# Clamp inside the adding instruction and half-size products for tokens 1024 to 1535, in a windowed-attention and two-layer kernel

## The chip, the core and the metric

The kernel runs on one core of one Trainium2 chip. The engines that it uses are PE (TensorE: matrix products and transposes), DVE (VectorE), ACT (ScalarE), POOL (GpSimd, here only for issuing loads that convert to bf16) and SP (SyncE, here for issuing transposing transfers and stores). They run side by side, each through its own list of instructions in order, and wait for each other by semaphores. The metric is the device time of one execution in microseconds (us). Lower is better.

## The reference

Attention in a window of 32 positions to either side, for 8 batches of 8 heads, 576 positions and 64 values a head; then two dense layers over the 4608 tokens of width 512, with a squared relu between them.

```
scores = 1/sqrt(64) * q @ k^T ;  |i - j| > 32 masked out
attn = softmax(scores) ;  x = attn @ v          # x: 4608 tokens x 512
h = x @ w_in                                     # w_in 512 x 2048
g = max(h, 0) ** 2
out = g @ w_out                                  # w_out 2048 x 512
```

Inputs and output are fp32; the kernel computes in bf16 with fp32 sums.

## The kernel before

**Attention.** The tokens come in 24 groups G of 192 (three groups, g = 0 to 2, to a batch b). For each group POOL loads q and k (`load_qk`, line 377: the tile `raw`, four buffers, so that group G and group G + 4 use the same one) and v (`load_v`, line 415). q and k have to be turned, so that the head's 64 values lie across partitions. For G below `NTG` PE turns them (`turn_pe`, line 463: eight small transposes for k and eight for q) and DVE or ACT brings them from PSUM to the tile `kq`; for the others SP issues a transposing transfer from `raw` to `kq` (`turn_dma`, line 491: two for a group, `td` and the group's numbers in the names). Then `scores` (line 531, PE; for G below `NSPLIT` the two halves of a group are issued apart), the exponential on ACT (line 554), the mask on DVE (562), `pv` (line 590, PE: two halves `P..A` and `P..B` of eight matmuls each) with a reciprocal and a normalising product on DVE (604, 608), and `xturn`, which turns the result for the first layer: by PE for G below `NXT` (lines 630 and 636, four transposes each, and a copy into the tile `xt`), otherwise by two transposing transfers of SP (lines 649 and 652, `T..a` and `T..b`).

**First layer.** Tokens 0 to 1023 go in tiles of 192 or 256 tokens through `mm1` (line 690). Tokens 1024 to 1535 (`PAIR`) go through `mm1` too, 16 outputs of 128 features for all 512 tokens at once, each of four matmuls of 512 columns; two outputs share two PSUM banks, one relu of 1024 elements a partition and one square of 1024. From 1536 on (`MM1S`) each set of 512 tokens goes through `mm1s`. There the product is split in two by two by two and made by seven products of half the size in place of eight (Strassen's scheme in Winograd's form). Four blocks m of features, each: seven products of four matmuls of 256 columns (line 770, named `Q<token>.<m><product>`), a seed copy within PSUM (line 809), four evictions by ACT or DVE (two relus, two plain copies to fp32 tiles `oe`), two adds of PSUM and such a copy (line 794), a clamp of both sums at zero (lines 800, 801) and squares (lines 659, 660) that write the tile `gt`. The products need sums of quarters of w_in (tile `sw`, made once, line 730) and differences of quarters of `xt` (tile `xs`, four per token set, line 742).

**Second layer.** Tokens 0 to 511 go by plain matmuls (`mm2`, line 835). The later sets of 512 go by seven products as well (`strassen`, line 917: products of 16 matmuls of 256 columns, named `P<set>.<product><half>`), with sums of `gt` on DVE (line 885), copies and adds (669, 670, 949) and stores that SP or ACT issues (847, 848).

**What sets the order.** A planner outside the kernel has given every operation a start number in nanoseconds; the long text `ORDER` holds them in the order in which the operations are recorded, with a letter for the engine (P for PE, A for ACT, D for DVE, G for POOL, S for SP), and after them the buffer of each tile. `apply` sorts by these numbers. The kernel does not wait for the times; only the order within each engine, the engine chosen and the buffer follow from them. Many operations may be given to ACT or to DVE. `fill` puts small idle matmuls in front of PE's early work (line 299). `OPEN` lists the first loads.

Of the kernel before, what the change touches and what calls it, by code (L numbers as in the profile page):

```python
# [2 lines left out]

# [12 lines left out]
RING = 1536  # L16
# [5 lines left out]
    MM1S=(1536, 2048, 2560, 3072, 3584, 4096),  # L22
# [8 lines left out]
    NTG=9,  # L31
# [3 lines left out]
    NXT=9,  # L35
    NSPLIT=6,
# [20 lines left out]
    ALTB=300,  # L57
)
# [174 lines left out]
class Gen:  # L233
# [7 lines left out]
    def alloc(self):  # L241
# [159 lines left out]
    def load_v(self, b, g, key, after=None):  # L401
        G, NV = 3 * b + g, self.cfg["NV"]
        vt = self.V[G % NV]
        for j in range(2):
            k0 = 192 * g - 32 + 128 * j
            lo, hi = max(k0, 0), min(k0 + 128, S_)
            if self.vcopy(G) and j == 0:
                lo += 64
                vs, vf = self.V[(G - 1) % NV][64:128, 1, :, 0:64], vt[0:64, 0, :, 0:64]
                self.p.rec("DVE", lambda e, vs=vs, vf=vf: e.tensor_copy(vf, vs), reads=[("v", (G - 1) % NV, 1)], writes=[("vc", G % NV)],  # L410
# [322 lines left out]
    def mm1s(self, t0, key):  # L733
# [5 lines left out]
        b11, b12, b21, b22 = xt[:, 0:2, r:r + 256], xt[:, 0:2, r + 256:r + 512], xt[:, 2:4, r:r + 256], xt[:, 2:4, r + 256:r + 512]  # L739
        for i, a, b, rd in ((0, b12, b11, st[0] + st[1]), (1, b22, xs[0][:], st[1] + [("xs", 0)]),  # L740
                            (2, b22, b12, st[1]), (3, b21, xs[1][:], st[0] + [("xs", 1)])):
            p.rec("DVE", lambda e, o=xs[i][:], a=a, b=b: e.tensor_tensor(o, a, b, ALU.subtract), reads=rd, writes=[("xs", i)],
                  key=key, dur=dve(512), name=f"xs{i}.{t0}")
        tag = lambda f, h: [("gt", (t0 // 64 + 4 * h + x) % (GRING // 64), d) for x in range(4) for d in f]
        for m in range(4):
# [46 lines left out]
            def fused(src, tg, u, y, kk, nm, hh=hh, add=add):  # L792
                hs = lambda y=y: self.rt(hh)[:, 512 * y:512 * y + 512]
                add.append(p.rec("DVE", lambda e: e.tensor_tensor(hs(), src(), self.oe(u), ALU.add), reads=[tg, u],  # L794
                                 writes=[(hh, y)], key=kk, dur=dve(512, False), name=nm, uses=[v, hh], after=add[0] if y else None))
                if y or not cfg["FP"]:
# [3 lines left out]
                    p.rec("DVE", lambda e: e.tensor_scalar(src2(), src2(), 0.0, None, ALU.max), reads=rd, writes=rd, key=kk, dur=153 + 0.26 * c,  # L800
# [6 lines left out]

            prod(1, ks[0])
# [3 lines left out]
            one(X, xtag, rt, lo, ks[1], f"{t0}.{m}")  # L812
# [53 lines left out]
    def sums_g(self, g, key):  # L866
# [3 lines left out]
        for c in (0, 1, None):  # L870
            whole = c is None
            if whole and not cfg["S34"]:
                continue
# [5 lines left out]
            for n, o, a, b, op, rd, wr in ((1, s1, a21, a22, ALU.add, t21 + t22, [("s", 0, c)]),  # L879
                                           (2, s2, s1, a11, ALU.subtract, [("s", 0, c)] + t11, [("s", 1, c)]),  # L880
                                           (3, a21, a11, a21, ALU.subtract, t11 + t21, t21),
                                           (4, a12, a12, s2, ALU.subtract, sr + t12, t12)):
                if cfg["S34"] and whole != (n > 2):
                    continue
# [8 lines left out]
    def wash(self, e, v):  # L893
        if v.wash:
            e.matmul(self.bank(v, 1), self.ZZ[:, 0:128], self.ZZ[:, 0:512], start=True, stop=True)
# [30 lines left out]
    def strassen(self, g, key):  # L926
# [4 lines left out]
        u2, p5 = Virt("oe"), Virt("oe")  # L931
# [31 lines left out]
        out(0, 0, [xt], None, X, ks[1], f"c11.{g}")  # L963
        self.product(g, 6, ks[2], v)
# [124 lines left out]
G14196 G17484 G19880 G19100 A20153 G12716 G13408 G20660 G22228 P7128 D7733 P8149 D8701 P9323 A9958 D11076 P10902  # L1089
# [136 lines left out]
```

## Time and profile before

| | |
|---|---|
| three runs | 286.67, 287.23, 287.79 us (median 287.23) |
| profiled execution, first to last instruction | 287.0 us |
| granted PE clock | 0.999 in the mean |
| PE busy | 279.1 us, 97% |
| DVE busy | 238.0 us, 83% |
| ACT busy | 215.7 us, 75% |
| POOL busy | 115.0 us, 40% |
| DMA moved | 37.57 MB, 131 GB/s in the mean |

The profiled execution has no time of its own beside its span; the runs stand for it, with a median 0.2 us above the span. How to read it: the profile counts an instruction as busy from its start to its end. Matmuls overlap each other, so PE's busy time is no proof that it works at its full rate; the distance between matmuls is better. "L770" is line 770 of the kernel as it was. A line may stand for several operations where a helper issues them. In a group, the number after x counts instructions; then come busy microseconds and the mean nanoseconds of one, then the idle time of the engine ahead of them and who ended it. In the chain of waits each row has a start, a length and what ran.

### The profile page before, as it was taken

The page shows a single profiled execution, that of the slowest core. Times are in us where ns is not written, and L with a number is a line of the kernel's source. Part 1 is how long each engine was busy: PE and PEld are TensorE (multiplying, and loading weights), DVE is VectorE, ACT ScalarE, POOL GpSimd, SP SyncE. Part 2 cuts the span into 40 slices and gives each one's busy share as a digit, 9 for nine tenths or more (in the row PEclk, how much of TensorE's full clock was granted, in tenths as well). Part 3 has the DMA queues.
Part 4 walks back from the last instruction along what each step waited for, and adds up shares of the span by engine and source line. Part 5 has one row for each costly group of instructions (what it writes and reads, how often), then busy time and mean ns, then how long its engine had stood idle before and what let it go on. Part 6 is the DMA issues. An engine that isn't in the chain of part 4 may idle for free.

```text
span 287.0 us, 7773 instructions
## 1 busy us (share of the span) xinstructions
PE 279.1 (97%) x3137; PEld 234.6 (82%) x3151; DVE 238.0 (83%) x438; ACT 215.7 (75%) x328; POOL 115.0 (40%) x153
## 2 busy tenths in 40 slices
PE   8999999999999999998999999999999999999995
PEld 8879866787756688886898888888888888888884
DVE  4787797989887798996899989998989978898721
ACT  2787666857868787887887889988887688798620
POOL 8999867194498052076235912605000000000000
PEclk9999999999999999999999999999999999999999
DMA  9999999999999999999999996989941612200233
GB/s 143 165 193 185 204 173 156 156 113 152 119 158 175 190 112 147 190 115 163 163 154 134 151 166 144 132 180 118 145 98 46 130 34 61 75 0 2 73 112 110
DMA packets 162915, 37.57 MB, mean 131 GB/s; under 512 B 150080, under 2 KB 162368, under 8 KB 162880
## 3 DMA queue, kind: packets, MB, share of 16 engines
q0 software_dynamic: 113728, 17.93, 87.7%
q1 hardware_dynamic: 44432, 15.34, 29.8%
q10 hardware_dynamic: 4720, 3.80, 5.1%
q8 instruction: 25, 0.41, 0.6%
q14 instruction: 10, 0.08, 0.1%
HBM read 36.70 MB, written 9.44 MB: 161 GB/s over the span
## 4 chain that ended last, share of the span: by engine, by line
PE 78%; DMA 10%; POOL 6%; DVE 2%; issue 2%; ACT 1%; ACTq 0%; DVEq 0%; POOLq 0%
PE ps L917 31%; PE ps L770 24%; PE ps L690 9%; PE ps L835 4%; POOL raw L377 4%; PE ps L590 3%; DMA w<-in_moe_w_in_dram 3%; PE ps L531 3%; DMA kq<-raw 3%; DMA v<-in_v_dram 2%; POOL v L415 2%; DMA xt<-xa 2%; PE ps L463 1%; DVE rt L794 1%; PE ps L630 0%
## 5 line engine op out<-in xcount | busy, mean ns | idle before, releaser
L665 ACT ACTIVATE rt<-ps 128x512 bf16<-128x512 f32 (+2 forms) x81 | 48.4, 606 | 17.6 <-PE ps L690 7.3
L670 ACT ACTIVATE oe<-ps 128x512 f32<-128x512 f32 x72 | 42.0, 595 | 22.2 <-PE ps L917 15.1
L554 ACT ACTIVATE e<-ps 128x1024 bf16<-128x1024 f32 x48 | 48.8, 1022 | 6.8 <-PE ps L531 5.0
L377 POOL DMA_DIRECT2D raw<-in_q_dram x46 | 36.7, 809 | 42.3 <-DMA kq<-raw 39.0
L377 POOL DMA_DIRECT2D raw<-in_k_dram x46 | 36.8, 816 | 27.2 <-DMA kq<-raw 20.8
L917 PE MATMUL ps<-w,gt 128*128 128x256 bf16 x384 | 47.0, 273 | 0.0
L690 PE MATMUL ps<-xt,w 128*128 128x192 bf16 (+2 forms) x379 | 46.4, 271 | 0.6 <-DMA w<-in_moe_w_in_dram 0.2
L415 POOL DMA_DIRECT2D v<-in_v_dram x48 | 38.6, 814 | 12.4 <-ACT v L412 10.0
L917 PEld LDWEIGHTS ps<-w,gt 128*128 128x128 bf16 x384 | 36.6, 98 | 4.9 <-issue 0.2
L770 PE MATMUL ps<-xs,sw 128*128 128x256 bf16 x288 | 39.9, 272 | 0.0
L690 PEld LDWEIGHTS ps<-xt,w 128*128 128x128 bf16 x384 | 32.4, 98 | 8.8 <-ACT v L412 0.3
L659 ACT ACTIVATE gt<-rt 128x512 bf16<-128x512 bf16 (+2 forms) x51 | 38.7, 777 | 0.3
L794 DVE TENSOR_TENSOR rt<-ps,oe 128x512 bf16<-128x512 f32 x48 | 32.9, 688 | 5.1 <-PE ps L770 3.8
L917 PE MATMUL ps<-ts,gt 128*128 128x256 bf16 x256 | 31.9, 273 | 0.0
L562 DVE TENSOR_TENSOR pt<-e,mask 128x2048 bf16<-128x2048 bf16 (+1 forms) x30 | 30.2, 1007 | 1.9 <-ACT e L554 1.4
L917 PE MATMUL ps<-ts,ss 128*128 128x256 bf16 x256 | 31.7, 273 | 0.0
L770 PEld LDWEIGHTS ps<-xs,sw 128*128 128x128 bf16 x288 | 27.4, 98 | 3.3 <-ACT oe L670 0.2
L770 PE MATMUL ps<-xt,w 128*128 128x256 bf16 x192 | 27.2, 273 | 0.2
L917 PEld LDWEIGHTS ps<-ts,ss 128*128 128x128 bf16 x256 | 24.7, 98 | 3.2
L660 DVE TENSOR_TENSOR gt<-rt 128x1024 bf16<-128x1024 bf16 (+2 forms) x49 | 26.4, 557 | 0.8 <-ACT rt L665 0.7
L917 PEld LDWEIGHTS ps<-ts,gt 128*128 128x128 bf16 x256 | 24.5, 98 | 3.2 <-DVE oe L949 0.3
L770 PEld LDWEIGHTS ps<-xt,w 128*128 128x128 bf16 x192 | 18.1, 98 | 3.3 <-ACT ps L809 0.4
(70 smaller groups left out, 405.2 us busy)
## 6 DMA issues: line engine op xcount, KB each, us to landing
out_dram<-oe SPq DMA_DIRECT2D x23, 256.0 KB, 3.5
out_dram<-oe ACTq DMA_DIRECT2D x13, 256.0 KB, 4.4
v<-in_v_dram POOLq DMA_DIRECT2D x16, 128.0 KB, 5.5
w<-in_moe_w_in_dram POOLq DMA_DIRECT2D x4, 512.0 KB, 9.8
w<-in_moe_w_out_dram POOLq DMA_DIRECT2D x4, 512.0 KB, 16.4
raw<-in_q_dram POOLq DMA_DIRECT2D x18, 96.0 KB, 5.3
raw<-in_k_dram POOLq DMA_DIRECT2D x14, 112.0 KB, 5.3
raw<-in_q_dram POOLq DMA_DIRECT2D x14, 112.0 KB, 6.9
```

The lines of the kernel that those rows point to most:

```text
L377: self.p.rec("POOL", lambda e, j=j, dst=dst: e.dma_start(dst, s[j]), writes=[self.rtag(t, b, g, j)], dma=(f"{t}{G % self.cfg['NRAW']}{j}", ...
L415: self.p.rec("POOL", lambda e, j=j, lo=lo, hi=hi, k0=k0: e.dma_start(vt[lo - k0:hi - k0, j, :, 0:64], self.v[b, :, lo:hi, :].rearrange("h ...
L554: last = self.p.rec("ACT", lambda e, ef=ef, v=v: e.activation(ef(), self.bank(v, 0, 2), ACTF.Exp, scale=0.125), reads=[v], writes=tags, ke ...
L562: self.p.rec("DVE", lambda e, pf=pf, ef=ef, mb=mb, n=n: e.tensor_tensor(pf(y=0, n=n), ef(y=0, n=n).rearrange("p (w h q) -> p w h q", w=n, ...
L659: alt = ("ACT", act(c), lambda e: e.activation(dst, src(), ACTF.Square)) if self.cfg["ALT"] else None
L660: self.p.rec("DVE", lambda e: e.tensor_tensor(dst, src(), src(), ALU.mult), reads=rd, writes=wr, key=key, dur=dve(c), name=name, alt=alt, ...
L665: return self.p.rec("ACT", lambda e: e.activation(dst(), src(), ACTF.Relu), reads=rd, writes=wr, key=key, dur=act(c), name=name, alt=alt, ...
L670: self.p.rec("ACT", lambda e: e.activation(dst(), src(), ACTF.Copy), reads=rd, writes=wr, key=key, dur=act(c), name=name, alt=alt, bias=se ...
L690: mm = e.matmul(ht[:, n * x:n * x + n], self.W1[:, ft, 128 * d:128 * d + 128], self.XT[:, ft, r:r + n], start=(ft == 0 and x == 0), stop=( ...
L770: mm = e.matmul(bk[:, 256 * x:256 * x + 256], lhs(k, 256 * m + 128 * x), rhs[:, k, :], start=start and x == 0 and k == 0, stop=(k == 1), s ...
L794: add.append(p.rec("DVE", lambda e: e.tensor_tensor(hs(), src(), self.oe(u), ALU.add), reads=[tg, u], writes=[(hh, y)], key=kk, dur=dve(51 ...
L917: mm = e.matmul(op[:, 256 * y:256 * y + 256], lhs[:, l0[0] + k, a:a + 128], rhs[:, r0 + k, c0:c0 + 256], start=start and y == 0 and k == 0 ...
```

## The change

Five things change at once.

1. The two adds of a block of `mm1s` become one instruction each that adds, takes the smaller of the sum and a huge constant, and the larger of that and zero (`TENSOR_ADD_SAT`, a DVE instruction that is not among the built-in ones; key `AS`). The separate clamp goes.
2. The squares of a block are made two at a time (`ZP`): the first relu together with the first add, the second add together with the second relu, 1024 elements each, in place of one of 1024 and two of 512. The first and third `xs` difference become one instruction (`XM`); the four `xs` tiles lie in one tensor for this.
3. Tokens 1024 to 1535 go through `mm1s` too.
4. Group 8, the ninth, is turned by transposing transfers in place of PE, its q and k as well as its result (`NTG`, `NXT` 8 in place of 9). Groups 3, 4 and 5 no longer have their halves of the scores apart (`NSPLIT` 3 in place of 6).
5. `ORDER` is new throughout; its planner took the times at which transfers land from a fit to measured ones. POOL's iota, which ran first, comes after five loads.

The other new keys (`VD`, `WIDE`, `JT`, `JM`) are off, and the code under them is not run; `SH` is 1, which leaves `sums_g` as it was.

```diff
-    MM1S=(1536, 2048, 2560, 3072, 3584, 4096),
+    MM1S=(1024, 1536, 2048, 2560, 3072, 3584, 4096),
...
-    NTG=9,
+    NTG=8,
...
-    NXT=9,
-    NSPLIT=6,
+    NXT=8,
+    NSPLIT=3,
...
+    AS=1,
+    ZP=1,
+    XM=1,
...
-            self.XS = [sb(f"xs{i}", [128, 2, 256], BF16) for i in range(4)]
+            self.XSA = sb("xs", [128, 4, 2, 256], BF16)
+            self.XS = [self.XSA[:, (0, 2, 1, 3)[i], :, :] for i in range(4)]
...
+        if cfg["XM"]:
+            both = [bass.AP(xt, o, [[4 * RING, 128], [x, 2], [RING, 2], [1, 256]]) for o, x in ((r + 256, 2 * RING), (r, 256))]
+            p.rec("DVE", lambda e: e.tensor_tensor(self.XSA[:, 0:2, :, :], both[0], both[1], ALU.subtract), reads=st[0] + st[1],
+                  writes=[("xs", 0), ("xs", 2)], key=key, dur=dve(1024), name=f"xs0.{t0}")
...
+            def pair(z, y, src, tg, u, kk, nm, held, v=v, lo=lo, hi=hi):
+                zf = lambda: self.rt(z)[:, 512 * y:512 * y + 512]
+                if u is None:
+                    held.append(self.relu(zf, src, [tg], [(z, y)], kk, "r" + nm, 512, uses=[v, z], after=held[0] if y else None))
+                else:
+                    held.append(p.rec("DVE", lambda e: e._custom_dve(TENSOR_ADD_SAT, out=zf(), in0=src(), in1=self.oe(u), s0=3.4028234e38, s1=0.0),
+                                      reads=[tg, u], writes=[(z, y)], key=kk, dur=dve(512, False), name=nm, uses=[v, z], after=held[0] if y else None))
+                if y:
+                    o = 256 if u is None else 0
+                    dst = bass.AP(gt, lo[0] * GRING + rg + o, [[16 * GRING, 128], [(hi[0] - lo[0]) * GRING + 256 - 2 * o, 2], [GRING, 2], [1, 256]])
+                    self.square(lambda: self.rt(z).rearrange("p (y d t) -> p y d t", y=2, d=2), dst, [(z, 0), (z, 1)],
+                                tag(lo, int(o > 0)) + tag(hi, int(o == 0)), kk, "g" + nm, 1024, uses=[z])
...
             prod(2, ks[1])
-            one(X, xtag, rt, lo, ks[1], f"{t0}.{m}")
+            if cfg["ZP"]:
+                pair(za, 0, X, xtag, None, ks[1], f"{t0}.{m}", ha)
...
-            fused(Y, ytag, p5, 0, ks[4], f"c22.{t0}.{m}")
+            if cfg["ZP"]:
+                pair(za, 1, Y, ytag, p5, ks[4], f"c22.{t0}.{m}", ha)
...
-            fused(X, xtag, u2, 1, ks[5], f"c12.{t0}.{m}")
+            if cfg["ZP"]:
+                pair(zb, 0, X, xtag, u2, ks[5], f"c12.{t0}.{m}", hb)
...
-            one(Y, ytag, rt2, hi, ks[6], f"{t0}.{m}b")
+            if cfg["ZP"]:
+                pair(zb, 1, Y, ytag, None, ks[6], f"{t0}.{m}b", hb)
...
 ORDER = """
-D900 G1350 A1170 D2200 D5546 D9773 D10213 D10698 D7178 D9553 D11762 D7058 D7598 D10413 D11962 D9453 D5746 D17653 D5256
-D4966 D1100 D1800 D9993 D10808 D2000 D7378 D9253 D18439 D38379 D42315 D48333 D30870 D48923 S1350 D6458 S900 D4366
-G2488 G1700 G4852 G3276 G5640 G4064 G6428 G7956 A1600 A8036 A2050 A7416 G7168 G9388 A14797 G8696 G11052 G10272 G11936
...
-P124317 D124787 D125673 S122484 S146618 D130056 D131580 D130475 D132684 P134709 A135356 P136047 D137330 A144849
...
+D850 G4790 A4935 D5640 D7566 D8656 D8946 D10715 D5240 D5860 D11377 D9146 D9266 D1340 D1910 D14529 D2110 D21824 D7766
+D10225 D1050 D6080 D7246 D10515 D5440 D10005 D19244 D21424 D1625 D7466 D2010 D12184 D43970 S850 D6646 S1300 D8056 G850
+G1638 G2426 G3214 G5140 G4002 G5928 G7456 A5365 A10079 A850 A4315 G6668 G9080 A16455 G9964 G8196 G10656 G11436 G12908
...
+P118690 A119337 P119127 A119938 P120438 D121109 P121962 D122857 A127543 P122399 D124227 P124164 A125139 D126815
...
+D110931 S109557 S124289 G71879 G76847 G71091 G75271 D102613 G98064 G93143 P105129 A105989 A107107 D108225 S84473
...
+S117366 S132445 D132990 D133745 D134364 P134853 A135778 P136629 A137581 P137066 A138182 P138637 A139384 P139074
...
+D140263 A144192 P140385 D141032 P141259 A142389 D147315 P136192 A138783 P139511 A141788 P139948 A141187 P142570
```

More of the change, by code (lines that the diff above doesn't have):

```diff
@@ L2 @@
 from concourse import mybir
+from concourse.dve_ops import TENSOR_ADD_SAT
 ALU = mybir.AluOpType
@@ L57 @@
     ALTB=300,
+    AS=1,
+    VD=0,
+    ZP=1,
+    XM=1,
+    WIDE=(),
+    JT=0,
+    JM=0,
+    SH=1,
 )
@@ L871, in sums_g @@
             whole = c is None
-            if whole and not cfg["S34"]:
+            if whole and not cfg["S34"] or not whole and not cfg["SH"]:
                 continue
@@ L894, in wash @@
         if v.wash:
-            e.matmul(self.bank(v, 1), self.ZZ[:, 0:128], self.ZZ[:, 0:512], start=True, stop=True)
+            for i in range(v.n // 2, v.n):
+                e.matmul(self.bank(v, i), self.ZZ[:, 0:128], self.ZZ[:, 0:512], start=True, stop=True)
     def product(self, g, i, key, v):
```

348 lines of the change are left out of this document (243 added, 105 removed), and 9 rows, old and new, of the table ORDER.

## The prediction

> **What bounds the kernel now.** I read the page's first two parts, then busy time by stages, then the chain of waits in order of time.
>
> ```profile
> span 287.0 us, 7773 instructions
> PE 279.1 (97%) x3137; PEld 234.6 (82%) x3151; DVE 238.0 (83%) x438; ACT 215.7 (75%) x328; POOL 115.0 (40%) x153
> ...
> DMA  9999999999999999999999996989941612200233
> ```
>
> ```profile
> 20.00:76.00 56.00, 55.46 (x712) 44.85 (x717) 48.28 (x96) 40.75 (x64) 36.53 (x49) 1.00 1.86 161
> 76.00:98.00 22.00, 21.35 (x209) 14.00 (x213) 17.95 (x30) 16.19 (x20) 16.04 (x21) 1.00 1.92 152
> 98.00:130.00 32.00, 31.74 (x345) 26.36 (x344) 28.87 (x50) 26.93 (x40) 12.84 (x17) 1.00 1.36 153
> 130.00:134.00 4.00, 2.67 (x24) 1.94 (x22) 2.52 (x6) 2.48 (x4) 3.74 (x5) 1.00 2.42 153
> 134.00:270.00 136.00, 135.76 (x1439) 118.61 (x1440) 122.17 (x210) 114.64 (x183) 26.85 (x35) 1.00 0.86 108
> 270.00:284.00 14.00, 13.62 (x125) 11.90 (x123) 4.99 (x7) 2.56 (x5) 0.00 (x0) 1.00 0.29 97
> ```
>
> The columns are the stretch, its length, then busy microseconds of PE, PEld, DVE, ACT and POOL with their instructions, the granted clock, the DMA share and GB/s. From 20 us on PE is busy almost without a break, at a granted clock of 1.00. Only 130 to 134 is open, with 2.67 of 4. A busy PE can hide waits, so the chain has to confirm it.
>
> ```profile
> 11.65 9.21 DMA w<-in_moe_w_in_dram
> ...
> 20.99 0.82 PE ps L690 x8
> ...
> 24.71 0.25 PE ps L590 x8
> 24.96 0.22 PE ps L630 x4
> ...
> 27.16 0.39 PE ps L463 x8
> 27.56 0.23 PE ps L636 x4
> ...
> 33.46 0.33 PE ps L531 x8
> ```
>
> ```profile
> 37.84 2.59 PE ps L835 x12
> ...
> 50.88 0.55 PE ps L531 x16
> ...
> 85.01 6.26 DMA v<-in_v_dram
> ...
> 92.60 0.43 PE ps L590 x8
> ...
> 126.16 5.83 DMA xt<-xa
> 132.17 0.49 DVE xs L742 x2
> ...
> 133.59 0.61 PE ps L770 x4
> ...
> 246.94 9.61 PE ps L770 x88
> ...
> 283.71 0.60 ACT oe L670
> ```
>
> Three parts stand out. Up to 21 us loads set the time: the second quarter of w_in is issued at 11.65 and lands at 20.86. From there PE leads, with two breaks: about 0.6 us, by my estimate, before 92.60, where the v transfer that lands at 91.27 leads through ACT to PE; and 1.6 us before 133.59, where the last turned piece of tokens 2048 to 2559 took 5.83 us to land and the xs differences and an add followed it on DVE. From 134 on PE is followed by PE. The last copy ends at 284.3; the remaining 2.7 us to 287.0 are the last store, of which the change alters only the issuing queue (SP for ACT). So a microsecond of PE work is worth nearly a microsecond, as long as DVE and ACT (122.17 and 114.64 of 136 from 134 to 270, 90% and 84%) keep up.
>
> **The change part by part, PE.** Tokens 1024 to 1535 lose 64 matmuls of 512 columns (16 outputs by 4) and get 112 of 256 (4 blocks, 7 products, 4 each). From the chain: 12 of 512 columns in 2.59 us is 0.216 each, 64 make 13.8; 88 of 256 in 9.61 is 0.109 each, 112 make 12.2. That is -1.6. The row of 512 columns is the second layer's, with the same tile shape.
>
> Group 8 (the ninth) loses two turns of eight (0.39 each, rather less since its pieces are narrower) and eight transposes of x (0.22 and 0.23 for four): -1.1. Groups 3, 4 and 5 get both halves of their scores together: two times 0.33 become 0.55, -0.1 each, -0.3. PE together: **-3.0**.
>
> **DVE and ACT.** The rows, kept apart by shape:
>
> ```profile
> L794 DVE TENSOR_TENSOR rt<-ps,oe 128x512 bf16<-128x512 f32 x48 | 32.9, 688 | 5.1 <-PE ps L770 3.8 <-ACT oe L670 0.4 <-ACT gt L659 0.2
> L665 ACT ACTIVATE rt<-ps 128x512 bf16<-128x512 f32 x50 | 29.4, 594 | 8.6 <-PE ps L770 7.0 <-PE ps L690 1.2
> ...
> L562 DVE TENSOR_TENSOR pt<-e,mask 128x2048 bf16<-128x2048 bf16 x18 | 21.9, 1219 | 1.5 <-ACT e L554 1.2
> L659 ACT ACTIVATE gt<-rt 128x512 bf16<-128x512 bf16 x30 | 18.3, 627 | 0.2
> L659 ACT ACTIVATE gt<-rt 128x1024 bf16<-128x1024 bf16 x15 | 15.7, 1053 | 0.1
> L660 DVE TENSOR_TENSOR gt<-rt 128x1024 bf16<-128x1024 bf16 x21 | 14.2, 683 | 0.0
> L801 ACT ACTIVATE rt<-rt 128x1024 bf16<-128x1024 bf16 x8 | 8.4, 1055 | 1.0 <-DVE rt L794 1.0
> L665 ACT ACTIVATE rt<-ps 128x1024 bf16<-128x1024 f32 x8 | 8.2, 1023 | 2.5 <-PE ps L690 2.4
> L660 DVE TENSOR_TENSOR gt<-rt 128x512 bf16<-128x512 bf16 x18 | 7.2, 417 | 0.0
> L800 DVE TENSOR_SCALAR rt<-rt 128x1024 bf16<-128x1024 bf16 x16 | 6.9, 440 | 0.2
> L742 DVE TENSOR_TENSOR xs<-xt,xs 128x512 bf16<-128x512 bf16 x12 | 5.0, 418 | 0.1
> ```
>
> The clamp inside the add takes away all 24 clamps: 6.9 us on DVE, 8.4 on ACT. The new instruction is in no row. Its bounds: 0.688, an add of the same operands, if the clamp costs nothing; 0.688 + 0.440 if it costs what the clamp did. A gain on the add I exclude, since it still reads 512 fp32 elements from the same two places. I take 0.688, the row it is nearest to: same inputs, output and count.
> [...]
>
> The squares of the other six token blocks: 48 of 512 elements (7.2 on DVE, 18.3 on ACT) become 24 of 1024, at 0.683 or 1.053 (16.4 to 25.3): 0 to 9 us less. The first and third xs difference become one of 1024: twice 0.418 against about 0.683, 0.15 a block.
>
> Tokens 1024 to 1535 go the other way. Removed: 8 relus of 1024 (8.2) and 8 squares (0.683 to 1.053 each). Added, a block: five evictions of 512 (seed, two relus, two copies) at 0.594, two adds at 0.688, two squares; four blocks and 1.5 for xs make 24.4 (squares on DVE) or 27.3. The stage gets **10.7 us more** work for the two engines. From 76 to 98 they stand idle for 4.05 and 5.81, 9.9 in all, so most of it fits; before that come more idle (7.7 and 15.2 from 20 to 76) and after it the savings above. I count it at nothing; its price, if that cover is gone, is the first rival.
>
> **A new wait that I read from the order.** In the new ORDER, between Q1536.0's product 5 and Q2048.1's product 5 (start numbers P120438 to P142570), PE gets 42 first-layer products and no second-layer product in between; the longest such run before has 22, the 88 matmuls of 9.61 us above, with no attention in it. A second-layer product is 16 matmuls with few evictions, so it is what gives DVE and ACT time. In the run PE has 42 x 0.437 + 2 x 0.55 (scores) + 3 x 0.26 (three half PVs, 0.25 in the chain), 20.2 us. ACT is given 25 evictions (0.594), 4 exponentials (1.02, by the 1024-element relu) and 3 squares (1.053): 22.1. DVE is given 17 of 512 from PSUM (0.688), 9 of 1024 (0.683), two of 2048 (1.22) and small ones of 1.7: 22.0. So PE waits about **+2.0** there, with bounds 0 (work left over for later) and 4 (the two engines also wait for each other).
>
> **Waits that go.** Why was that piece late before 133.59? SP issues in order, and issued it late:
>
> ```profile
> 124.83 2.58 SPq L649 DMA_TRANSPOSE xt<-xa  x2
> ```
>
> Transposes of keys and queries stand ahead of it; from 124.83 to 127.41 SP issues the last two x pieces, the very last some 3.4 us behind the start number of the last one (122.48). In the old ORDER 7.6 us lie between the last piece (122.48) and the first xs difference on it (130.06); in the new one 8.7 (T11b at 124.29, xs0.2048 at 132.99). With the same lateness and the slowest landing, 3.4 + 5.83 = 9.2, about 0.5 us of the 1.6 stay. The 0.6 at 92 goes too, since the v loads there are ordered anew. That is -2.2 for both, bounds -2.2 and 0, and **+0.5** for what stays or opens elsewhere, bounds 0 and 2.2.
>
> **DMA queues.** Group 8 costs SP four more transposes. Behind them on SP are the transposes of group 9 and stores; behind the raw buffer that is now released by a landing and not by PE are POOL's loads of group 12.
>
> ```profile
> POOL raw L377 <- DMA kq<-raw: 59.8, 7, 13.7
> ```
>
> ```profile
> kq<-raw SPq DMA_TRANSPOSE x30, 4.4
> ```
>
> POOL already waits 59.8 us for such landings without PE being late for more than the two breaks, and both pieces of group 8 are turned some 8 us before its scores, with a landing of 4.4. I take 0; bounds 0 and 2.7 (a landing of 4.4 that is not covered, less the 1.7 of a second-layer product, sixteen times 0.109, that PE could take instead).
> [...]
>
> **The opening.** POOL's iota moves behind five loads, and one more v load ahead of w_in's first quarter. The gating second quarter keeps 13 loads and the iota ahead of it, so it leaves about as before; the first quarter has one load more ahead of it, and one issue of POOL is 5.59/7 = 0.8 us by the row below. I take 0, bounds -0.5 (the iota's place no longer delays the first loads) and +0.8.
>
> ```profile
> 1.39 5.59 POOL raw L377 x7
> ```
>
> **Sum:** -3.0 + 2.0 - 2.2 + 0.5 = -2.7, on the profiled span of 287.0: 284.3. The median of the runs, 287.23, is 0.2 over that span, so the median after is 284.5; I say **284.4**.
>
> **The rivals.**
> 1. DVE and ACT become the bound from 76 to 98. For it: the 10.7 us against 9.9 idle; the fullest stretches above keep DVE at 90%. Even at 95%, the most that I grant them, there is room for 0.95 x 44 - 34.1 = 7.7, so 3.0 are over, 1.5 on each engine. Against: work can be drawn ahead and behind. Time: 284.4 + 1.5 = 285.9, within 0.5% of before.
> 2. Landings: a late one takes the place of each removed, and the uncovered landing of group 8 comes on top. 284.4 + 2.7 = 287.1, no change. For it the DMA row; against it that all but two landings were covered before.
> 3. Slower: the new instruction costs what add and clamp cost, 0.44 more. From 134 to 270 there are 40 such adds (five token blocks): 17.6 more, less the 5.8 of the clamps gone from DVE (40 of 48 in 6.9), 11.8. DVE has 13.8 idle there, 7.0 if it fills to 95%, so 4.8 are over and PE waits for them: 284.4 + 4.8 = 289.2. By the run of 42 alone, with 10 adds on a full DVE, it is slower than before from 0.28 us an add (10 x 0.28 = 2.8). Nothing in the rows speaks for it but that the instruction is unknown; against it, that its inputs and output are those of the add.
> 4. The half-size products save PE nothing because each set costs an extra gap. Against: 88 of them stand in 9.61 without one. PE gets back 1.6: 286.0.
>
> **How the numbers follow.** Forecast 0.74, first rival 0.09, second 0.08, third 0.05, fourth 0.04. About 0.5%, 1.4 us, is what a measurement of this kernel can tell from no change. The forecast's own spread, from the opening (-0.5, +0.8), the run of 42 (0 to 4) and the landings (0 to 2.2), reaches from 282.8 to 286.3 and is mostly below 285.8; some of it falls within 0.5%, and so do rivals one, two and four in the main. Faster 0.75, same 0.19, slower 0.06. The range, taking in the first and fourth rival and nearly the second: 283.0 to 286.7.
>
> **What would show it.** Right: 256-column matmuls of the first layer's line number 784 in place of 672, none of 512 columns there; 56 new adds near 0.69 us; no clamps; a PE gap of about 2 us in all between 120 and 144 behind DVE or ACT; from 145 on PE after PE, some 2.5 us earlier than before. Wrong: adds over 0.8 us, a PE released by a DMA for over a microsecond after 25 us, or first-layer matmuls in 76 to 98 that wait for copies and adds.

## The result, and the profile after

The changed kernel is slower. Its median is 293.67 us (290.69 to 295.88, four runs) against 287.51 (286.67 to 288.30) for the kernel before in the same comparison; the ratio is 1.0148, 95% interval 1.0100 to 1.0195. Here and below a ratio leaves out runs more than 1.5% above the fastest of their kernel (295.25 and 295.88 here, so that 291.39 is the median of the rest), and it need not be the quotient of the two medians. The prediction was 284.4 (283.0 to 286.7), faster. The profiled execution has a span of 290.3 us and a time of 292.09.

From the page after (busy totals, the clock and the DMA engines by slices of a fortieth of the span, a group of section 5), and busy time by the stages that were shown of before:

```profile
span 290.3 us, 7825 instructions
...
PE 277.1 (95%) x3183; PEld 238.9 (82%) x3183; DVE 236.5 (81%) x413; ACT 211.4 (73%) x316; POOL 114.6 (39%) x153
...
PEclk9999999999999999799999999999999999999999
DMA  9999999999999999999999999996411321300133
...
L844 DVE CUSTOM_DVE_ANT_0 rt<-ps,oe 128x512 bf16<-128x512 f32 x56 | 37.3, 687 | 6.7 <-PE ps L796 4.3
```

```profile
20.00:76.00 56.00, 56.00 (x728) 45.24 (x726) 47.87 (x88) 46.18 (x72) 44.25 (x58) 1.00 1.97 170
76.00:98.00 22.00, 21.52 (x231) 18.71 (x230) 20.03 (x32) 18.08 (x30) 13.26 (x18) 1.00 1.84 157
98.00:130.00 32.00, 27.74 (x339) 23.49 (x337) 23.29 (x38) 20.59 (x29) 15.23 (x20) 0.95 1.71 171
130.00:146.00 16.00, 13.82 (x150) 11.41 (x148) 14.24 (x26) 13.95 (x23) 6.31 (x9) 1.00 1.78 161
146.00:270.00 124.00, 124.00 (x1303) 109.44 (x1302) 110.69 (x178) 97.74 (x146) 16.73 (x22) 1.00 0.80 96
```

PE has 2.0 us less busy time and the new add costs what a plain add cost, 687 ns. The loss lies between 98 and 146 us, where PE stands idle for 6.4 of 48 us. In the kernel before it was 1.7: 0.3 from 98 to 130, and the rest in the row below.

```profile
130.00:146.00 16.00, 14.54 (x159) 12.33 (x157) 13.55 (x24) 12.72 (x21) 8.21 (x11) 1.00 1.78 168
```

After the change, the chain of waits names what PE waited for, and the waits give its size:

```profile
75.34 16.41 DMA v<-in_v_dram
91.75 0.02 issue
91.78 0.63 ACT v L428
...
106.38 0.43 SPq L665
106.81 0.04 issue
106.86 1.58 SPq L668
...
108.55 8.94 DMA kq<-raw
117.49 0.14 issue
117.62 1.04 PE ps L547 x16
...
141.37 1.03 ACT e L570
```

```profile
PE ps L547 <- DMA kq<-raw: 4.3, 1, 4.3
...
PE ps L796 <- ACT e L570: 1.5, 1, 1.5
...
PE ps L606 <- DMA v<-in_v_dram: 0.6, 2, 0.4
```

The scores of group 14 wait 4.3 us for keys and queries that SP issues at 108.55, behind two x pieces, and that land 8.94 us later. What the granted clock does after this wait stands in windows of 2 us:

```profile
114.00:116.00 2.00, 0.00 (x0) 0.00 (x0) 0.00 (x0) 0.00 (x0) 0.30 (x1) 1.00 1.43 232
116.00:118.00 2.00, 0.38 (x8) 0.41 (x10) 0.00 (x0) 0.00 (x0) 0.00 (x0) 0.81 1.45 229
118.00:120.00 2.00, 2.00 (x26) 1.56 (x22) 0.22 (x1) 1.70 (x4) 1.29 (x2) 0.50 1.49 214
120.00:122.00 2.00, 2.00 (x17) 1.64 (x16) 1.87 (x5) 1.97 (x3) 0.21 (x1) 0.83 1.58 163
```

When PE comes back, the granted clock is 0.50 for 2 us and 0.83 for the next 2: 0.50 x 2 + 0.17 x 2 = 1.3 us of work lost on top of the wait. I set the start of every PE operation against its start number in `ORDER`, less some 0.3 us throughout. The lag is 0.0 to 0.2 us up to 90, 0.7 at 100, 6.3 at 120, 7.1 at 150, and 7.0 at the end; in the kernel before it is 1.3 at 150 and 1.2 at the end. So the new order promised 283.3 where the old one promised 285.8. It kept step for 90 us and then lost 0.5 for a v load, 5.6 for group 14 (4.3 and the clock) and 0.8 near 140, where PE waits for ACT.

The loads and the transposes of the attention land later than before. From the DMA issues (last number: median us from issue to landing), before (4.4 for `kq<-raw`, by the prediction's row) and then after:

```profile
raw<-in_q_dram POOLq DMA_DIRECT2D x18, 96.0 KB, 5.3
...
xt<-xb SPq DMA_TRANSPOSE x15, 4.0
```

```profile
raw<-in_q_dram POOLq DMA_DIRECT2D x18, 96.0 KB, 12.7
v<-in_v_dram POOLq DMA_DIRECT2D x16, 96.0 KB, 12.8
kq<-raw SPq DMA_TRANSPOSE x32, 8.0
...
xt<-xb SPq DMA_TRANSPOSE x16, 6.7
```

Counted from the issue and landing times of the two traces, 2 to 9 transfers are under way between 65 and 145 us before, sampled each 5 us, and 11 to 18 after. From 50 to 140 us POOL issues 57 loads before and 71 after, SP 27 and 32 transposes. By the start numbers, a load stands 12.6 us (50 to 100) and 16.3 us (100 to 150) ahead of its first use in the old order, in the median, and 15.8 and 31.0 in the new one.

### The profile page after: what moved, and what is told of

Read it like the earlier page. It is cut to its first block, busy times and chain, and to the rows that moved or that the text cites. A ratio compares the mean times of both kernels' runs of the same rounds, so it can differ in the third digit from the quotient of the medians.

```text
span 290.3 us, 7825 instructions
## 1 busy us (share of the span) xinstructions
PE 277.1 (95%) x3183; PEld 238.9 (82%) x3183; DVE 236.5 (81%) x413; ACT 211.4 (73%) x316; POOL 114.6 (39%) x153
## 3 DMA queue, kind: packets, MB, share of 16 engines
q0 software_dynamic: 113728, 17.93, 88.1%
## 4 chain that ended last, share of the span: by engine, by line
PE 75%; DMA 15%; POOL 4%; ACT 2%; issue 1%; DVE 1%; SPq 1%; POOLq 0%; ACTq 0%
PE ps L1091 30%; PE ps L796 26%; PE ps L706 7%; DMA kq<-raw 6%; DMA v<-in_v_dram 6%; PE ps L1007 4%; PE ps L606 3%; PE ps L547 3%; DMA w<-in_moe_w_in_dram 3%; POOL raw L387 3%; POOL v L431 1%; PE ps L479 1%; ACT e L570 1%; SPq L668 1%; ACT rt L681 1%
## 5 line engine op out<-in xcount | busy, mean ns | idle before, releaser
L686 ACT ACTIVATE oe<-ps 128x512 f32<-128x512 f32 x78 | 45.4, 594 | 29.1 <-PE ps L1091 12.2
L681 ACT ACTIVATE rt<-ps 128x512 bf16<-128x512 f32 (+1 forms) x82 | 44.6, 560 | 13.3 <-PE ps L796 6.9
L570 ACT ACTIVATE e<-ps 128x1024 bf16<-128x1024 f32 x48 | 48.7, 1021 | 4.2 <-PE ps L547 1.9
L675 ACT ACTIVATE gt<-rt 128x1024 bf16<-128x1024 bf16 (+1 forms) x43 | 43.1, 1011 | 4.6 <-DVE rt L680 2.3
L796 PE MATMUL ps<-xs,sw 128*128 128x256 bf16 x336 | 45.9, 273 | 0.2 <-ACT rt L681 0.2
L844 DVE CUSTOM_DVE_ANT_0 rt<-ps,oe 128x512 bf16<-128x512 f32 x56 | 37.3, 687 | 6.7 <-PE ps L796 4.3
L796 PEld LDWEIGHTS ps<-xs,sw 128*128 128x128 bf16 x336 | 31.9, 98 | 4.4 <-ACT rt L681 0.5
L706 PE MATMUL ps<-xt,w 128*128 128x192 bf16 (+1 forms) x320 | 31.9, 252 | 1.0 <-DMA w<-in_moe_w_in_dram 1.0
L796 PE MATMUL ps<-xt,w 128*128 128x256 bf16 x224 | 31.3, 273 | 1.5 <-ACT e L570 1.5
L706 PEld LDWEIGHTS ps<-xt,w 128*128 128x128 bf16 x320 | 26.6, 97 | 2.6 <-ACT e L570 1.4
L796 PEld LDWEIGHTS ps<-xt,w 128*128 128x128 bf16 x224 | 21.2, 97 | 4.5 <-ACT e L570 1.8
L676 DVE TENSOR_TENSOR gt<-rt 128x1024 bf16<-128x1024 bf16 (+1 forms) x33 | 21.2, 656 | 0.3 <-ACT rt L681 0.2
## 6 DMA issues: line engine op xcount, KB each, us to landing
v<-in_v_dram POOLq DMA_DIRECT2D x16, 128.0 KB, 12.7
raw<-in_q_dram POOLq DMA_DIRECT2D x18, 96.0 KB, 12.7
raw<-in_q_dram POOLq DMA_DIRECT2D x14, 112.0 KB, 12.7
```

What stands on the lines that cost most here:

```text
L570: last = self.p.rec("ACT", lambda e, ef=ef, v=v: e.activation(ef(), self.bank(v, 0, 2), ACTF.Exp, scale=0.125), reads=[v], writes=tags, ke ...
L675: alt = ("ACT", act(c), lambda e: e.activation(dst, src(), ACTF.Square)) if self.cfg["ALT"] else None
L676: self.p.rec("DVE", lambda e: e.tensor_tensor(dst, src(), src(), ALU.mult), reads=rd, writes=wr, key=key, dur=dve(c), name=name, alt=alt, ...
L681: return self.p.rec("ACT", lambda e: e.activation(dst(), src(), ACTF.Relu), reads=rd, writes=wr, key=key, dur=act(c), name=name, alt=alt, ...
L686: self.p.rec("ACT", lambda e: e.activation(dst(), src(), ACTF.Copy), reads=rd, writes=wr, key=key, dur=act(c), name=name, alt=alt, bias=se ...
L706: mm = e.matmul(ht[:, n * x:n * x + n], self.W1[:, ft, 128 * d:128 * d + 128], self.XT[:, ft, r:r + n], start=(ft == 0 and x == 0), stop=( ...
```

## The experiments

| | kernel | median us (range) | ratio to before, 95% | load of q, kq |
|---|---|---|---|---|
| | changed kernel | 293.67 (290.69 to 295.88) | 1.0148 (1.0100 to 1.0195) | 12.7, 8.0 |
| 1 | plain add, no clamp | 294.38 (290.79 to 297.74) | 1.0193 (1.0094 to 1.0291) | 9.3, 7.3 |
| 2 | before, clamping add | 286.69 (286.24 to 288.92) | 0.9982 (0.9958 to 1.0006) | 5.1, 4.8 |
| 3 | a transpose earlier on SP | 294.25 (292.96 to 297.03) | 1.0243 (1.0157 to 1.0329) | 13.6, 7.5 |
| 4 | rows of 512 values | 297.92 (293.45 to 302.64) | 1.0224 (1.0124 to 1.0323) | 9.6, 8.0 |
| 5 | before, rows of 512 values | 287.17 (286.80 to 288.08) | 0.9987 (0.9957 to 1.0018) | 5.4, 4.6 |
| 6 | at most 7 loads under way | 293.21 (292.53 to 294.46) | 1.0203 (1.0151 to 1.0256) | 7.1, 7.1 |
| 7 | at most 4 | 301.90 (299.40 to 303.06) | 1.0489 (1.0420 to 1.0558) | 5.4, 5.5 |
| 8 | half the rows from group 12 on | 284.87 (283.74 to 286.13) | 0.9907 (0.9878 to 0.9936) | 6.4 (half), 6.8 |
| 9 | before, half the rows | 286.90 (286.72 to 287.86) | 0.9983 (0.9960 to 1.0006) | 3.1 (half), 4.5 |
| 10 | before, group 8 by transposes | 291.99 (290.82 to 293.27) | 1.0157 (1.0101 to 1.0213) | 5.6, 4.1 |
| 11 | group 8 on PE | 288.77 (287.52 to 292.83) | 1.0046 (0.9997 to 1.0095) | 10.9, 8.1 |
| 12 | only group 8's result on PE | 294.59 (290.04 to 296.86) | 1.0158 (1.0085 to 1.0231) | 12.3, 8.4 |
| 13 | loads paced 14 us ahead | 291.73 (290.10 to 293.43) | 1.0144 (1.0099 to 1.0188) | 6.2, 7.6 |
| 14 | paced 14, group 8 on PE | 286.64 (286.27 to 287.82) | 0.9991 (0.9974 to 1.0009) | 5.8, 6.4 |
| 15 | paced 11, group 8 on PE | 286.89 (286.23 to 287.79) | 0.9996 (0.9980 to 1.0011) | 5.8, 6.0 |
| 16 | paced 14, only keys and queries on PE | 292.15 (289.21 to 292.94) | 1.0167 (1.0095 to 1.0238) | 5.4, 6.8 |
| 17 | as 14, with four idle transposes | 288.36 (287.02 to 294.21) | 1.0022 (0.9985 to 1.0059) | 6.5, 6.9 |

The last column has the medians from issue to landing of the 96 KB loads of q and of the transposes of keys and queries. The kernel before ran beside each set, with medians from 286.8 to 287.6.

**1 and 2. Is it the new instruction?** In 1 it becomes a plain add, and the clamp of these sums is left out:

```diff
-held.append(p.rec("DVE", lambda e: e._custom_dve(TENSOR_ADD_SAT, out=zf(), in0=src(), in1=self.oe(u), s0=3.4028234e38, s1=0.0),
+held.append(p.rec("DVE", lambda e: e.tensor_tensor(zf(), src(), self.oe(u), ALU.add),
```

> The changed kernel, with a plain add in place of the instruction that adds and clamps; the clamp of the two sums is left out, so the output is another. Same order. If the new instruction costs nothing (theory L and Q), the span is that of the changed kernel, 289 to 291, with the same wait before S14B. [...] If it slows DVE (theory V), the span falls below 287.

In 2 the kernel before gets the clamping add alone (`AS` 1; the clamps' numbers are taken out of its `ORDER`):

> The kernel before, in its own order, with one part of the change: the add that clamps, and no clamps; nothing else is moved. Theory B: the loss is not in the adds; 6.9 us go from DVE and 8.4 from ACT where PE seldom waits for them, and loads and transposes stay as they were; time 286.3 to 287.6, the stalls at 92 and 133 as before. If the new instruction had a price beside its 687 ns (a later start, a slower neighbour), it would be over 288.5.

Without the new instruction the changed kernel is as slow, and with it the old one is no slower. PE waits for transfers in 1 as in the changed kernel:

```profile
PE ps L547 <- DMA kq<-raw: 3.4, 1, 3.4
...
PE ps L606 <- DMA v<-in_v_dram: 2.9, 2, 2.3
```

In the old kernel it also gains nothing measurable (the interval takes in 1); apart from the 1.3 us near 132, which began with a late x piece, PE waited for DVE or ACT for 0.8 us there after the opening, in the larger rows.

**3. Is it the place of one transpose on SP?** The number of the late one is lowered, so that it goes ahead of the two x pieces and a store:

```diff
-S102555
+S98000
```

> The changed kernel, with one start number changed: group 14's second transposing transfer (td421) goes to SP right behind td420, ahead of a store and of the x pieces T10a and T9b. Theory L (SP's order lets a late x piece hold back a transfer that PE needs): td421 is issued near 104 in place of 108.3, lands near 113, and PE's wait of 4.5 us before S14B shrinks to 0 to 1; the clock does not drop behind it; span 285 to 286.5, time less by the same 4 to 5 us. Theory Q (the landing is late because the loads and transfers are too many for the 16 engines, whatever SP's order): td421 lands at 115 or later, or the next transfer is late in its place, and the span stays at 288 or more.

Its wait fell to 0.6, but the time did not. PE then waits 4.0 us for a copy on ACT whose buffer hung on a store, and 2.5 us for xs; in the chain a store and an x piece take the place of the keys:

```profile
109.41 8.54 DMA out_dram<-oe
...
133.28 9.59 DMA xt<-xb
```

So it is not the place of this one transfer: here, moving it ahead made two others late.

**4 and 5. Is it the number of packets?** The loads of groups 9 to 23 read rows of 512 consecutive values, the same bytes (the gathering by head is left out; the loads of v, not shown, are changed alike). Of the DMA queues only q0 changes, from 113,728 packets to 73,408 with 17.93 MB as before. Packets under 512 B fall by 46,080, which is the number of rows of 64 values in these groups' q and k alone (2 x 8 x 15 x 192), so not all the packets that I meant to save were saved:

```diff
+        if 3 * b + g >= 9:
+            flat = src.rearrange("h s d -> (h s d)").rearrange("(r c) -> r c", c=512)
+            return [flat[t0 + n // 2 * j:t0 + n // 2 * j + n // 2, :].rearrange("p (h d) -> p h d", h=8) for j in range(2)], n // 2
...
```

> The changed kernel, but for groups 9 to 23 the loads of q, k and v read 512 consecutive values a position in place of 64 values from each of the 8 heads: the same bytes in an eighth of the packets, so the gathering of the heads is left out from there on and the output is another. Theory L and theory Q alike: without late landings the order runs as its numbers say, PE's waits before S14B and P9B go, span 283 to 284.5; what then remains against the forecast of 284.3 is the vector engines' wait near 132 to 142 (2 us, kept). Theory V (vector engines or the new instruction slow the kernel): span stays at 288 or more.

> The kernel before, with the same lighter loads for groups 9 to 23 (gathering of the heads left out there). It shows what landings cost the old order: theories L and Q expect the two breaks of 0.6 and 1.6 us to go, span 285 to 286. The difference to the changed kernel with the same loads is then the change without landings: 1.5 to 2.5 us in favour of the changed kernel.

The median landing of q's loads is 9.6 in place of 12.7, but it was 9.3 in 1, whose loads are those of the changed kernel, so this shows no gain. In its profiled execution, the longest of its four (302.64), the scores wait longer:

```profile
PE ps L551 <- DMA kq<-raw: 7.9, 2, 7.4
```

With 40,320 packets fewer in q0 the time does not fall, so the packet count alone is not the cause. 5 shows something about the kernel before: its waits at 92 and 133 are gone, and the median falls by 0.4 only, which is not clear of noise.

**6 and 7. A limit on loads under way.**

```diff
+        loads = [o for o in self.out if o.eng == "POOL" and o.dma and o.name[0] in "qkv" and o.start > 40000]
+        for a, b in zip(loads, loads[7:]):
+            b.deps.add(a)
```

> The changed kernel, with one more wait: from 40 us of the plan on, each load of q, k or v that POOL issues waits until the load seven places earlier has landed, so that at most seven loads are under way. Nothing else differs. Theory B (backlog: the new order issues loads so far ahead that 11 to 18 transfers are under way from 55 to 145 us, and an urgent load or transpose waits behind those that are not urgent): loads land in 5 to 8 us in place of 12.7 to 13.5, the 4.3 us wait of PE before the scores of group 14 falls under 1.5, and the time is 284 to 287.5. Rival G (the four more transposes of group 8, and the denser order on SP, are the load that the queues can't bear): landings of loads get shorter, but PE still waits over 3 us for transposes between 90 and 125, time over 290. Rival V (the 10.7 us more of vector work from 76 to 98 delays what comes after): time unchanged, 291 to 294, with PE's waits on DVE and ACT.

> As the kernel with at most seven loads under way, but with four. Theory B: landings of 4 to 6 us; with a landing of about 5 and four under way POOL moves a load each 1.25 us, and 71 loads between 50 and 140 us in the new order need one each 1.27 us, so this is at the edge: some loads come late again, time 285 to 291, and the best limit lies between 4 and 13. Rivals G and V: 290 or more.

Loads land faster, in 7.1 and 5.4 us, but they are issued later, and PE waits longer: in 6 for v 2.9 us, for keys and queries 2.8 and for xs 1.9. With four under way the landings are near those of the kernel before (5.3 and 4.4), and it is the slowest kernel of all, because PE waits for v:

```profile
PE ps L609 <- DMA v<-in_v_dram: 11.1, 4, 3.7
```

So the backlog is not only a matter of issuing too much ahead. My reading is that in the new sequence on POOL loads needed next stand behind others, and that a limit alone holds both back; 13 to 16 change the sequence too. My theory of the backlog alone fell here.

**8 and 9. Fewer bytes.** The same instructions, order and waits, half the rows:

```diff
-            self.p.rec("POOL", lambda e, j=j, dst=dst: e.dma_start(dst, s[j]),
+            c = h // 2 if G >= 12 else 0
+            self.p.rec("POOL", lambda e, j=j, dst=dst, c=c: e.dma_start(dst[c:], s[j][c:]),
...
+            lo = lo + n // 2 if G >= 12 else lo
```

> The changed kernel with each load of q, k and v of groups 12 to 23 cut to half its rows (the other half keeps what an earlier group left, so the output isn't the reference's): the same instructions, order and waits, about half the bytes and packets of these loads. Theory D: loads land in under 7 us from 80 us on, PE's waits between 90 and 145 us fall from about 8 to under 3 (the 2 us behind DVE and ACT near 140 stay), time 284 to 287, and 1.5 to 3 us under the kernel before with the same cut. Theory G: landings of transposes stay at 6 to 8 us, time over 289.

> The kernel before with the same loads of groups 12 to 23 cut to half their rows (output not the reference's). Both theories: the waits of 0.6 us at 92 and 1.6 at 133 shrink, landings of 4 to 5 us, time 285.5 to 287; it is what the changed kernel with half loads is to be compared with.

This is the decisive pair. Without late transfers the changed kernel takes 284.87, and it is 2.0 us faster than the old one with the same cut; no run of the one is as long as any of the other. Its lag behind the start numbers is at most 0.4 us from 80 us on and -0.2 at the end. The half loads take POOL a little less time to issue too (from 60 to 200 us 0.70 us for one of q or k, in place of 0.78), but in 4, where that fell to 0.53, nothing was gained. Windows of 8 and then 9:

```profile
98.00:130.00 32.00, 32.00 (x396) 27.73 (x394) 28.49 (x47) 25.68 (x37) 16.28 (x25) 1.00 1.72 179
130.00:146.00 16.00, 14.93 (x156) 12.46 (x154) 14.92 (x26) 14.86 (x25) 5.57 (x9) 1.00 0.97 109
```

```profile
98.00:130.00 32.00, 31.75 (x347) 26.57 (x345) 28.84 (x50) 26.96 (x40) 13.11 (x20) 1.00 1.10 123
130.00:146.00 16.00, 15.88 (x173) 13.75 (x171) 15.03 (x27) 13.89 (x22) 3.89 (x6) 1.00 1.13 118
```

**10 to 12. Group 8.** In 10 the old order gets the four transposes (`NTG` and `NXT` 8; start numbers 65.9 and 66.0, 89.5 and 89.6), and two of group 8's loads change places with one of group 10 and one of group 11. In 11 the changed order has group 8 back on PE (`NTG` and `NXT` 9; one load of group 12 changes places with one of v), in 12 its result only (`NXT` 9).

> The kernel before, in its own order, with one part of the change: group 8 turned by four transposes on SP in place of PE (keys and queries at 66 us of the plan, the result at 89.5); two of its loads change places with two of group 11, so that they land in time. Theory B: the transposes by themselves cost little. PE loses 1.1 us of work, landings stay at 4.4 to 6, PE waits at most 1 us more; time 286 to 288. Rival G: landings go up by half or more, PE waits 2 us or more for transposes between 75 and 110, time over 289.

> The changed kernel with group 8 back on PE: its two transposes of keys and queries and the two of its result go from SP (start numbers 58.9, 60.9, 85.8, 88.3), PE turns them as in the kernel before (64.1, 67.0, 95.2, 95.4), the first load into its raw buffer changes places with one of v. PE gets 1.1 us more. Theory G (what the four transposes take of SP and of the queues is most of the loss, as in the kernel before with group 8 alone, 291.99): the wait before the scores of group 14 falls under 2 us, time 285 to 288. Theory D (the new order as a whole asks for 71 loads and 32 transposes between 50 and 140 us where the old one asks for 57 and 27, more than the queues land in that time): the wait stays over 3 us or moves to another transfer, time 290 to 294.

> The changed kernel with only the result of group 8 turned by PE (start numbers 95.2, 95.4), its keys and queries by SP as in the change. It says which two of the four transposes cost: if those of the result, which SP issues at 86 and 88 us ahead of a dense stretch, the time is near that with all of group 8 on PE (287.5 to 290); if those of keys and queries, which free the buffers ten us earlier for further loads, it stays at 291 to 294. Theory D expects the second, theory G either.

Four transposes cost the old order 4.8 us, though PE has less to do. Landings stay as they were in the median (5.6, 4.1); one does not. Near there a transpose into xt takes SP 1.3 to 2.3 us to issue; a later x piece is issued at 103.0 in place of 102.2, and takes 6.75 us to land where it took 2.34:

```profile
102.82 0.17 SPq L668
102.99 0.04 issue
103.03 6.75 DMA xt<-xa
```

PE then waits 3.7 us, and after that the clock falls to 0.50 as it does in the changed kernel. The places on SP were mine, so this shows what the four can cost, not what they must. In the changed order they cost about 3 us, by the ratios (1.0148 against 1.0046). With group 8 on PE, what is left is one wait for a v load,

```profile
PE ps L606 <- DMA v<-in_v_dram: 3.7, 2, 2.8
```

after which the clock stays at 1.00. Landings there are hardly shorter than in the changed kernel (10.9 and 8.1 us for 12.7 and 8.0). 12 stays where the changed kernel was: there the two transposes of keys and queries are enough.

**13 to 16. Pacing.** POOL's loads are sorted by first use, each set 14 (or 11) us of start numbers ahead of it, and held by a DVE instruction:

```diff
+        held = [o for o in self.out if o.eng == "DVE"]
+        for o in self.out:
+            if o.eng == "POOL" and o.dma and o.name[0] in "qkv" and o.start > 47000:
+                o.deps.add([g for g in held if g.start < o.start - 500][-1])
...
```

> The changed kernel, group 8 by transposes as there, with POOL's loads from 47 us of the plan on put in the order in which they are needed, each 14 us of the plan ahead of its first use (or when its buffer is free, if that is later), and held until the DVE instruction that stands just ahead of that time is done; everything else as it was. In the changed kernel's order they stand 16 us ahead in the median from 50 to 100 us and 31 us from 100 to 150 (12.6 and 16.3 in the order before). Theory D (loads issued too far ahead make the backlog that the urgent ones wait behind): landings 5 to 8 us, PE's waits between 90 and 125 us under 2, time 284.5 to 287. Theory G (the four transposes of group 8 are the load too many, whenever loads are issued): over 289.

> Group 8 on PE and the loads paced in the same way, 14 us ahead. Theory D: the 3.1 us wait for a v load that the kernel with group 8 on PE alone still has near 122 us goes, time 284.5 to 286.5, under both kernels. Theory G: no better than group 8 on PE alone (288.8).

> As that, with the loads 11 us ahead. Theory D: landings shorter still, 4 to 6 us, but less time for them; time 284 to 288, and the comparison with 14 says on which side of the best distance they stand. Theory G: 288 or more.

> Group 8's keys and queries on PE, its result by SP's two transposes as in the change, loads paced 14 us ahead. PE gets 0.5 us less than with all of group 8 on PE. If the two transposes of keys and queries are what costs: 286 to 287, no slower than with all of it on PE (286.64). If those of the result cost too: over 288.

With group 8 on PE, pacing brings the loads to 5.8 us, and no wait of PE for a transfer after 25 us is left among the larger ones. It is 1.6 us faster than 11, by the ratios, and level with the kernel before, no faster: PE has the 1.1 us of group 8 again. With group 8, or only its result, by transposes, a v load of group 12, issued at 102 or 103, takes 14.0 to 17.7 us to land, and PE waits for it; in 14 the same load, issued at 103.6, takes 7.5. In 16 the two transposes of the result are enough for that. The chain of 13, and its windows:

```profile
102.75 17.70 DMA v<-in_v_dram
```

```profile
116.00:118.00 2.00, 0.00 (x0) 0.00 (x0) 0.00 (x0) 1.40 (x2) 0.00 (x0) 0.76 1.60 159
118.00:120.00 2.00, 0.00 (x0) 0.00 (x0) 0.00 (x0) 0.00 (x0) 0.00 (x0) 0.50 1.43 242
```

11 us ahead is no worse than 14, so with group 8 on PE the landings are not at an edge. In 16 PE's wait and the clock behind it are

```profile
PE ps L610 <- DMA v<-in_v_dram: 2.4, 1, 2.4
...
118.00:120.00 2.00, 2.00 (x11) 1.44 (x10) 0.95 (x3) 0.26 (x1) 0.00 (x0) 0.50 1.36 266
```

**17. The traffic of four transposes alone.** As 14, with four transposes on SP at the places of group 8's, from w_in into parts of xt that are read no more.

> Group 8 on PE, loads paced 14 us ahead, and on SP four transposes more, at the places at which the changed kernel has those of group 8 (58.9, 60.9, 85.8, 88.3): each turns 128 rows of 512 values of w_in into a part of xt that is read no more, and nothing waits for it but the later transpose that writes there. Theory T (the four cost by what they take of SP and of the queues): 289 to 292, like the paced kernel with group 8 by transposes (291.73), with landings of 8 to 12 us between 70 and 120. Theory R (what costs is that group 8's own keys and queries, buffers and result then hang on landings): as without them, 286.2 to 287.3, landings of 6 to 8.

Between the two expectations. Seven of ten runs lie at 287.0 to 289.2 and three at 293.3 to 294.2. The seven are not clearly longer than 14 (1.0022 with 0.9985 to 1.0059, against 0.9991). The profiled one is one of the three, and it waits for the same v load as 13 and 16:

```profile
PE ps L613 <- DMA v<-in_v_dram: 4.5, 1, 4.5
```

That the traffic alone brings the three about is possible, but not shown; in the others its price is not clear of zero. With group 8's data hanging on the transposes (13, 16) no run is under 289.2. How much of the 5 us is traffic and how much the buffers and results that then hang on landings stays open, and so does why a few transposes in some sixty lengthen the loads for 40 us.

## Why the prediction was wrong, point by point

**PE, -3.0: right.** The matmuls of 256 columns are 784 (336, 224, 112 and 112 in four groups). With the transfers out of the way (8 against 9) PE's idle time from 20 to 270 us is 1.76 against 0.39, and the span is 2.0 shorter, so its work is about 2.0 + 1.4 = 3.4 us less.

**The add at 0.688: right**, 687 ns over 56. The third rival (the clamp costs as before) falls: the clamp added nothing to the 688 ns of the plain add.

**Vector work from 76 to 98 at nothing: right.** DVE is busy 20.03 and ACT 18.08 of 22 us, and in 8 PE is busy for all of that stretch (22.00). The first rival falls, and the fourth with the PE step.

**The run of 42 products, +2.0: right in kind, somewhat large.** In 8 PE idles 1.07 us between 130 and 146, with DVE and ACT at 14.92 and 14.86 of 16; in the changed kernel it idles 2.18 there, 1.5 of it in the row `ACT e L570`.

**Waits that go, -2.2: failed, at its baseline.** The step took both waits from one profiled execution and set its span beside the median, "0.2 us above the span". But time exceeds span by 1.8 us in every later run of the kernel before that shows both (288.92 and 287.1, for one). By that, the profiled execution of before took about 288.8 and was a long one; a run of 287.0 has a span near 285.2. With the waits gone (5 and 9), the median falls by 0.4 to 0.6, and neither is clear of noise. Against the median the step was worth some 0.5, not 2.2, and with it the sum is -1.0 from the median, 286.2. With PE at -3.4, the run of 42 at 1.1 and nothing for late transfers it is 284.4, near the 284.87 of 8. That the forecast was 284.4 too is luck: one term too large by 1.7 stood against others that were 1.3 and 0.5 too pessimistic.

**What stays or opens elsewhere, +0.5 with bounds 0 and 2.2, and DMA queues, 0 with bounds 0 and 2.7: the steps that failed.** Together they came to about 6, by the lag against the start numbers: 0.5 at 92, 4.3 and the clock's 1.3 at 117. (The 0.8 near 140 belongs to the run of 42.) The four transposes of group 8, which the step on the queues took to cost nothing, cost 4.8 us in the old order (10), about 3 in the new one (11) and 5.1 with paced loads (13 against 14), PE's own 1.1 less work included. Both steps priced a late transfer with the landings of before (4.4 and 5.83). The old and new distance from transfer to use had been compared for one x piece alone (7.6 and 8.7 us), and the new one was longer. I did not count the loads that the new order issues (71 for 57) nor ask what that does to landings: 12.7 for 5.3, and 8.0 for 4.4. The upper bound of 2.7 was one uncovered landing at its old length. The stated spread was too narrow besides: the bounds of the opening, the run of 42 and the landings, added up, reach from 281.4 to 288.9, not from 282.8 to 286.3.

Against the step on the queues stood the second rival, with the DMA row at nine tenths through slice 24. It was right in direction: with two transposes more on SP (16 against 14), POOL's load of v for group 12 takes 14.0 us in place of 7.5. I let the cover of before outweigh it.

**The second rival** (landings, 287.1, chance 0.08) was nearest to the mechanism, with a price of 2.7 for what measured 6.5 (291.39 less 284.87). The landing that PE waited for longest was that of group 14, not of group 8, and the rival left out the clock. After the wait of 4.3 us the clock's loss of 1.3 adds nearly a third to the wait; the clock was 0.50 for a while after the 3.7 us of 10 and the 2.4 us of 16 too, and stayed at 1.00 after the 2.8 us of 11. So in these runs the length of the wait alone does not decide it; what does is not shown.

**The opening, 0: right**; the lag at 60 us is 0.2. Of the signs named for wrong, one came: a PE released by a DMA for over a microsecond after 25 us.

## What to carry to other kernels

In these runs a landing time was not a property of the transfer alone: loads of 96 KB took 5.3 us with 2 to 9 transfers under way and 12.7 with 11 to 18. The new order, made with fitted landing times, issues the loads of 100 to 150 us a median 31.0 us ahead of their use, in place of 16.3; that a planner with long landings issues earlier and so crowds the queue further is my reading, not shown. Before a landing from an old profile is used for a new order, count the transfers that each order issues per stretch, and test the new order once with fewer bytes: here one pair of runs told the loss of the transfers from the gain of the rest. And before a sum is made against a profiled span, check what its own execution took; a wait seen in one profile may be worth a quarter of that in the median.

## What was not expected of the hardware

Cutting the packets of q0 from 113,728 to 73,408 at the same bytes took no time off; the loads of half the rows landed in 6.4 us in place of 12.7. And the sixteen completions of a load drew apart: in the changed kernel, for loads of q, k and v issued between 60 and 120 us, the last came 3.3 to 4.1 us after the eighth (means of each 10 us), against 0.5 to 1.2 in the kernel before and 0.2 to 1.0 in 14. It is not one completion alone: the twelfth came 1.3 to 2.2 us after the eighth, against 0.1 to 0.4 in the kernel before. So some shares of each load were held up more than others for 60 us. What held them up is not shown.
